# Two linear-attention and two feed-forward layers: keys of two tiles from centred rows, and weight loads on other queues

## The chip, the cores and the metric

The kernel runs on one core of a Trainium2 chip. A core has five engines with instruction queues of their own: TensorE (PE in the profile) multiplies matrices, VectorE (DVE) and ScalarE (ACT) work on tiles element by element, GpSimd (POOL) does small element-wise work and issues DMAs, and SyncE (SP) here only issues DMAs. Each engine works through its queue in order and waits on semaphores. The metric is the device time of one execution in microseconds (us); lower is better.

## The reference

The input `x` is 2048 rows of 512 values in bfloat16. Four layers follow one another: attention (A), feed-forward (B), and the same two again with the same weights.

```python
def _A_ref(x, wqkv, wo):              # D = 512, H = 32 heads of 16
    q, k, v = split_heads(x @ wqkv)
    phi = lambda t: jnp.where(t > 0, t + 1, jnp.exp(t)) + 1e-6
    pq, pk = phi(q), phi(k)
    kv  = jnp.einsum("bhsd,bhse->bhde", pk, v)
    z   = jnp.einsum("bhsd->bhd", pk)
    num = jnp.einsum("bhqd,bhde->bhqe", pq, kv)
    den = jnp.einsum("bhqd,bhd->bhq", pq, z)[..., None] + 1e-6
    return merge_heads(num / den) @ wo

def _B_ref(x, w_gate, w_up, w_down):  # inner width 1792
    return (silu(x @ w_gate) * (x @ w_up)) @ w_down

x = x + _A_ref(_layernorm(x), A_wqkv, A_wo)
x = x + _B_ref(_layernorm(x), B_w_gate, B_w_up, B_w_down)
# and both lines once more
```

The layer norm takes the mean off each row and divides by the root of variance plus 1e-5; it has no weights. The attention has no mask over positions: every query sees the sums over all keys.

## The kernel before, in words

The rows are held on the chip as sixteen tiles of 128 rows (`X`), in four groups of four tiles. Layers are numbered 0 to 3; 0 and 2 are attention, 1 and 3 feed-forward. All weights are loaded once.

*How work is named and ordered.* The kernel first records operations with what they read and write, and each engine then gets its operations in an order written out by hand: `PROGRAM` is the order of TensorE in tokens, `ORDER` has one list for each other engine. Semaphore waits follow from the recorded reads and writes. A token has the layer, a letter and the tile or group. `0t0` transposes normalised tile 0 on TensorE, `0k0` makes its keys, `0g0` adds its outer product to the accumulators, `0z0` its keys' sum. `0q03` makes queries of group 0, columns 3, and `0d03` the part of the denominators that they give. `0v` turns the outer products into per-head key-value matrices and `0m0` multiplies them by Wo. `0r0` spreads 1/denominator of group 0 over the heads' columns by matmuls, and `0w3` is the output projection of tile 3. `1u011` is gate and up of group 0, column 11, and `1n3` the down-projection of tile 3. `S` is one filler matmul of 128 columns on zeros. In `ORDER` a name has the token, a dot and the step: `0x4.apply` is the normalisation of tile 4, `0k0.exp` a step of `phi` of its keys.

*Layer norm* (`ln`): statistics on VectorE (`stats`, `aggr`) or ScalarE (`stats`, `sq`, then `negm` on GpSimd), `vpe` (variance plus epsilon), `pow` (1/std, on GpSimd) and `apply` into `xnA` (layers 0 and 2) or `xnB`. `apply` is on VectorE, or on ScalarE with one more small step, `nmr`. The normalised tile is transposed into `xnT`: by DMA, issued by SP (`xT` in SP's list), or, for tiles named in `PE_T` with a `t` (in layer 0: tiles 0, 1, 2, 3 and 14), by four TensorE transposes (`xt_pe`, line 544) and a copy out of the accumulator (`xT` on VectorE, line 552).

*Keys and queries* (`k_proj`, `q_proj`, `phi`): four matmuls of 512 columns into one accumulator bank. `phi` then takes `exp` on ScalarE (line 563), `ts` (minimum with 1, plus 1e-6, line 568) on VectorE, and the maximum with the value plus 1. That is one VectorE pass from the accumulator (`phi`, line 575), or, for names in `ON_ACT`, `id1` on ScalarE (line 566) and a shorter VectorE pass (line 572).

*Sums and denominators*: the keys' sums are masked per head into `Zm` (line 615), with `mask`, whose three building steps stand on GpSimd (`i.c5`, `i.c6`, `i.c7`; the last is line 429). In layer 0 tile 12's keys go into the sum on VectorE (`0s`: a copy and two conversions), the others by matmuls (`z`). Every `d` token needs `Zm`. Its result is inverted on VectorE (`den`). It is then spread by TensorE (`rep_pe`, with four VectorE products of line 750), for groups with a `d` in `PE_T` (0d0, 0d2, 2d1), or by four ScalarE passes (`rep`), four DMA transposes on SP (`rT`) and four VectorE products (`pqn`, line 732).

*Weight loads.* Keys' weights come on ScalarE's queue, X and the queries' weights Wq on SP's. The rest are issued by GpSimd in this order: Wv, Wo, four pairs of Wg and Wu, and four parts of Wd. The first of them waits for all transposes by DMA of layer 0. GpSimd has four DMA semaphores in turn, so each load is issued only when the one four places earlier has landed. The last step of `mask`, `i.c7`, stands behind the fourteenth load in GpSimd's list.

Of the kernel before, what the change touches and what calls it, by code (L numbers as in the profile page):

```python
# [4 lines left out]
ACT = mybir.ActivationFunctionType  # L5
# [160 lines left out]
S S S S S S S S S S S S S S S S S S S S S S S S S S S S S S S S S S S S S S S S S 0t0 0k0 S S S S S S S S S 0t1 S S  # L166
S 0t2 S S S 0k1 0g0 S 0k2 0t3 0g1 S S S 0k3 0k4 0g2 0k5 0g3 0k10 S 0g4 0k9 0g5 0k6 0k7 0q03 0g10 0z0 0k8 0k15 0z4
0g7 0k13 0k12 0k11 0g9 0z2 0z10 0z9 0q11 0z3 0z5 0z8 0t14 0z15 0g6 0z13 0k14 0q02 0z7 0q10 0q01 0q00 0z1 0g11 0q12
0q21 0z14 0z6 0z11 0q13 0s 0d02 0d03 0d01 0d00 0g8 0q20 0d11 0q22 0g13 0d12 0d13 0d10 0q23 0d20 0g15 0g12 0g14 0d23
0d22 0d21 0q30 0v 0q31 0m0 0r0 0m1 0m2 0r2 0m3 0w3 0w2 0q33 0w1 0w0 0w5 0w11 0q32 0w7 0w6 0w9 0d33 0w8 0w4 0w10  # L170
1u011 1u007 1u005 1u008 1u002 1u006 0d31 0d32 1u012 1u003 1u013 0d30 1u010 1u004 1u000 1u110 1u001 1u009 1n3 0w14
1n0 0w12 1u106 1n1 1u102 1n2 1u107 1u204 0w13 1u101 0w15 1u111 2k2 1u109 1u105 1u103 1u104 1u108 2k0 1u100 2k1 2q00
1u112 1u113 2k3 1n7 1u209 1n6 1u211 1u205 1n4 1n5 1u213 1u200 1u303 1u202 1u203 2q10 1u301 1u208 1u309 1u304 1u206
1u212 2g0 1u201 1u311 1u302 2q11 1u305 1u207 1u310 2q01 1u308 2q03 1u312 2q02 1u210 1n11 1u313 2k4 1u300 1n8 1n10
1u306 1n9 1u307 2k8 1n14 2k7 2k10 2k5 2q21 1n15 2k6 2k9 2k11 1n13 1n12 2q12 2k15 2k14 2g3 2g5 2q20 2q22 2k13 2q23
2g2 2k12 2g7 2g6 2g14 2q13 2s 2d01 2g12 2d02 2g1 2d00 2d03 2d20 2d13 2d21 2q30 2d22 2d10 2d12 2d11 2g13 2q31 2g10
2d23 2g15 2g4 2g9 2g11 2g8 2r1 2q32 2v 2q33 2m0 2m1 2m2 2m3 2d31 2d30 2w0 2w1 2w2 2d32 2w3 2w6 2w5 2w11 2d33 2w4 2w8
2w7 2w9 2w10 3u008 3u000 3u009 3u013 3u010 3u004 3u003 3u005 3u007 3u103 3u110 3u108 3u012 3u002 3u001 3u006 3u104
2w13 3u011 3n3 3u100 2w12 3n2 3n0 3u106 3u105 2w14 3u107 3u111 3n1 3u102 3u109 3u112 3u101 3u113 3n6 3n4 3n5 3n7
3u200 3u201 3u202 3u203 3u204 2w15 3u205 3u206 3u207 3u208 3u209 3u210 3u211 3u212 3u213 3n8 3n9 3n10 3n11 3u300  # L180
3u301 3u302 3u303 3u304 3u305 3u306 3u308 3u307 3u309 3u310 3u311 3u312 3u313 3n12 3n13 3n14 3n15
# [4 lines left out]
i.ld i.ld1 0x2.stats 0x2.sq 0x5.stats 0x7.stats 0k0.exp 0x5.sq 0x10.stats 0x10.sq 0k1.exp 0x7.sq 0x12.stats 0k2.exp  # L186
0k2.id1 0x15.stats 0x9.apply 0k3.exp 0x11.stats 0k4.exp 0x12.sq 0k5.exp 0x11.sq 0x15.sq 0k10.exp 0k9.exp i.c 0k6.exp
0k7.exp 0k6.id1 0q03.id1 0q03.exp 0k8.exp i.c1 i.c2 0k15.id1 0k15.exp 0k13.exp 0k12.exp 0k11.exp 0k11.id1 0q11.exp
i.c3 0k14.exp 0k14.id1 0q02.exp 0q02.id1 0q10.exp 0q01.exp 0q10.id1 0q00.exp 0q00.id1 0q12.id1 0q21.id1 0q12.exp
0q21.exp 0q13.id1 0q13.exp 0q20.exp 0q22.exp 0q23.exp 0d1.rep 0d1.rep1 0G0.evac 0G2.evac 0G3.evac 0q30.exp 0q30.id1  # L190
0q31.exp 0d1.rep2 0q31.id1 0M2.evac 0M0.evac 0M1.evac 0M3.evac 0d1.rep3 1x3.sq 0q33.exp 1x2.sq 1x3.apply 0q33.id1
1x1.sq 1x0.sq 0q32.exp 1x5.sq 0q32.id1 1x11.sq 1x7.sq 1u011.tanh 1u007.tanh 1u005.tanh 1x6.sq 1x11.apply 1u008.tanh
1x6.apply 1u006.tanh 1u002.tanh 1x7.apply 1x9.sq 1u012.tanh 1x9.apply 1u003.tanh 1u013.tanh 1x4.sq 1u010.tanh
0d3.rep 0d3.rep1 1u004.tanh 1x8.sq 1u000.tanh 0d3.rep2 1u001.tanh 1u110.tanh 1u009.tanh 1x10.sq 1x8.apply 1u102.tanh
1u106.tanh 0d3.rep3 2x0.sq 1x14.sq 2x1.sq 1u107.tanh 2x2.sq 1u204.tanh 2x3.sq 1u101.tanh 1u109.tanh 2x1.apply
1u111.tanh 1x14.apply 2k2.exp 1u105.tanh 1u103.tanh 2k2.id1 1u104.tanh 2k0.exp 1u108.tanh 2k0.id1 2k1.exp 2k1.id1
1x15.sq 2q00.id1 1u100.tanh 2q00.exp 1u113.tanh 1u112.tanh 1u209.tanh 1x12.sq 2k3.exp 2x7.sq 2k3.id1 1u211.tanh
1x13.sq 1u205.tanh 2x6.sq 2x4.sq 1u213.tanh 1u200.tanh 2x5.sq 1u303.tanh 1u202.tanh 1u203.tanh 1u301.tanh 2q10.exp
1u208.tanh 2q10.id1 1u309.tanh 1u304.tanh 1u206.tanh 1u212.tanh 1u201.tanh 1u311.tanh 1u302.tanh 2q11.id1 1u305.tanh
2q11.exp 1u207.tanh 1u310.tanh 2q01.id1 2q01.exp 1u308.tanh 2q03.id1 2q03.exp 1u312.tanh 2q02.exp 1u210.tanh  # L200
2q02.id1 1u313.tanh 2x11.sq 2k4.id1 2k4.exp 2x8.sq 1u300.tanh 2x10.sq 1u306.tanh 2x9.sq 1u307.tanh 2x10.apply
2k8.exp 2k8.id1 2x14.sq 2k7.exp 2q21.id1 2k10.exp 2q21.exp 2k5.exp 2k10.id1 2k5.id1 2k11.exp 2k6.exp 2x15.sq 2k9.exp
2x14.apply 2x13.sq 2x12.sq 2k15.exp 2q12.exp 2k14.exp 2q12.id1 2k15.id1 2q20.id1 2q20.exp 2q22.id1 2k13.exp 2k13.id1
2q23.exp 2k12.exp 2q23.id1 2q22.exp 2q13.exp 2d0.rep 2d0.rep1 2q31.exp 2d0.rep2 2q30.exp 2d0.rep3 2d2.rep 2G0.evac
2G1.evac 2G3.evac 2q32.exp 2d2.rep1 2q32.id1 2d2.rep2 2M0.evac 2M1.evac 2M3.evac 2q33.exp 2q33.id1 2d2.rep3 3x0.sq
3x1.sq 3x2.sq 3x3.sq 3x6.sq 3x5.sq 3x11.sq 3u008.tanh 3x11.apply 3x4.sq 3u009.tanh 3u000.tanh 3x7.sq 3u013.tanh
3u010.tanh 2d3.rep1 3u004.tanh 3x7.apply 3u003.tanh 3x9.sq 3u007.tanh 2d3.rep 3u005.tanh 3u103.tanh 2d3.rep2
3u108.tanh 2d3.rep3 3u110.tanh 3u012.tanh 3x8.sq 3u002.tanh 3u006.tanh 3u104.tanh 3u001.tanh 3u011.tanh 3x13.sq
3u100.tanh 3u106.tanh 3u105.tanh 3u107.tanh 3u111.tanh 3u102.tanh 3x10.sq 3u109.tanh 3x12.sq 3u112.tanh 3u101.tanh
3u113.tanh 3u200.tanh 3u202.tanh 3u201.tanh 3u203.tanh 3x14.sq 3u204.tanh 3x15.sq 3u205.tanh 3u206.tanh 3u207.tanh  # L210
3u208.tanh 3x14.apply 3u209.tanh 3u210.tanh 3u211.tanh 3x12.apply 3u212.tanh 3u213.tanh 3u300.tanh 3u301.tanh
3u303.tanh 3u302.tanh 3u304.tanh 3u306.tanh 3u305.tanh 3u308.tanh 3u307.tanh 3u310.tanh 3u309.tanh 3u311.tanh
3u312.tanh 3u313.tanh
""",
    "dve": """
i.c 0x0.stats 0x0.aggr 0x0.vpe 0x1.stats 0x0.apply 0x1.aggr 0x3.stats 0t0.xT 0x4.stats 0x1.apply 0x4.aggr 0x3.aggr
0x9.stats 0x2.apply 0t1.xT 0k0.ts 0x9.aggr 0k0.phi 0t2.xT 0x3.apply 0x4.apply 0k1.ts 0k1.phi 0x6.stats 0x5.apply
0t3.xT 0x6.aggr 0k2.ts 0x7.vpe 0x10.apply 0x14.stats 0k2.phi 0x13.stats 0k3.ts 0x14.aggr 0k3.phi 0x6.apply 0x7.apply
0k4.ts 0x8.stats 0k4.phi 0k5.ts 0x8.aggr 0x14.vpe 0x8.vpe 0x12.apply 0k5.phi 0x13.aggr 0k10.ts 0x8.apply 0x15.vpe
0k10.phi 0x15.apply 0k9.ts 0k9.phi 0k6.ts 0x13.apply 0k7.ts 0k6.phi 0k7.phi 0x11.apply 0q03.ts 0k8.ts 0k8.phi  # L220
0q03.phi 0x14.apply 0k15.ts 0k13.ts 0k15.phi 0k13.phi 0k12.ts 0k12.phi 0k12.zs 0t14.xT 0q11.ts 0k11.ts 0q11.phi
0k14.ts 0s.zh 0k11.phi 0q01.ts 0k14.phi 0q01.phi 0q00.ts 0q02.ts 0q02.phi 0q10.ts 0s.zl 0q10.phi 0z.zm 0q00.phi
0q12.ts 0q12.phi 0q13.ts 0d0.den 0q13.phi 0d0.den1 0q20.ts 0q21.ts 0q20.phi 0q21.phi 0d1.den 0q22.ts 0d1.den1
0q22.phi 0d0.den2 0q23.ts 0q23.phi 0G1.evac 0d2.den 0d2.den1 0v.mask 0d1.pqn 0d2.den2 0r0.pqn 0r0.pqn1 0r0.pqn2
0r0.pqn3 0d1.pqn1 0q31.ts 0r2.pqn 0w3.res 0r2.pqn1 0w2.res 0r2.pqn2 0r2.pqn3 0w1.res 0w0.res 1x2.apply 0d1.pqn2
1x1.vpe 0d1.pqn3 1x1.apply 0q33.ts 0w5.res 0q30.ts 0q33.phi 1x0.apply 0w11.res 0w6.res 0w8.res 0w7.res 1x5.vpe
0w10.res 0w4.res 0w9.res 1x11.vpe 1x5.apply 1x7.vpe 1u011.gst 1u011.h 1u005.gst 1u007.gst 0q32.ts 0q31.phi 1x6.vpe
0q32.phi 1u007.h 1u008.gst 1u005.h 1u008.h 1u006.gst 1u002.gst 0q30.phi 1u002.h 1u012.gst 1u006.h 1u003.gst 1u012.h
0d3.den 0d3.den1 1x4.apply 1u003.h 1u013.gst 1u010.gst 1u013.h 1u004.gst 1u010.h 1u004.h 0d3.pqn 1u000.gst 1u001.gst
1u000.h 1u001.h 1u009.gst 1u009.h 0d3.pqn2 1u110.gst 1u110.h 1n0.res 0w12.res 1n3.res 0w14.res 1x8.vpe 1x10.apply  # L230
1u106.gst 1n1.res 0d3.pqn1 1n2.res 0d3.pqn3 1u106.h 1u102.gst 2x2.vpe 1u204.gst 1u102.h 2x2.apply 1u107.gst 1u107.h
# [58 lines left out]
}  # L290

PE_T = set("""
0t0 0t1 0t2 0t3 2d1 0d0 0t14 0d2
""".split())


# [11 lines left out]
def bass_interleave_layers__linear_attn_block__swiglu_ffn__prompt_kernel(  # L308
# [20 lines left out]
    with stack:  # L329
# [65 lines left out]
        r_pq = Ring(NPQ)  # L395
        r_xb = Ring(NXB)
        r_xt = Ring(NXT)
        r_den = Ring(3)
        r_rrep = Ring(2)
        r_RT = Ring(2)  # L400
        r_th = Ring(NTH)
# [519 lines left out]
```

## Time and profile before

| What | Before |
|---|---|
| Median of three runs | 441.09 us (440.77 to 442.0) |
| The profiled execution's own time | 440.77 us |
| Its span in the profile | 439.0 us |
| TensorE busy | 420.1 us, 96% of the span |
| VectorE busy | 294.5 us, 67% |
| ScalarE busy | 199.6 us, 45% |
| GpSimd busy | 79.5 us, 18% |
| Granted TensorE clock, mean | 0.992 |
| Moved by DMA | 22.57 MB, mean 51 GB/s |

The profile is of one execution. Times within it count from the start of its span; the execution's own time is 1.77 us longer than the span. The chain that ended last is followed back from the last instruction, at each step to what released it. "Granted clock" is the share of full speed that TensorE had. A DMA has an issue, on the queue of the engine that starts it, and a landing, when its semaphore says that the data is there.

### The profile page before, as it was taken

The page shows a single profiled execution, that of the slowest core. Times are in us where ns is not written, and L with a number is a line of the kernel's source. Part 1 is how long each engine was busy: PE and PEld are TensorE (multiplying, and loading weights), DVE is VectorE, ACT ScalarE, POOL GpSimd, SP SyncE. Part 2 cuts the span into 40 slices and gives each one's busy share as a digit, 9 for nine tenths or more (in the row PEclk, how much of TensorE's full clock was granted, in tenths as well). Part 3 has the DMA queues.
Part 4 walks back from the last instruction along what each step waited for, and adds up shares of the span by engine and source line. Part 5 has one row for each costly group of instructions (what it writes and reads, how often), then busy time and mean ns, then how long its engine had stood idle before and what let it go on. Part 6 is the DMA issues. An engine that isn't in the chain of part 4 may idle for free.

```text
span 439.0 us, 6322 instructions
## 1 busy us (share of the span) xinstructions
PE 420.1 (96%) x2201; PEld 196.7 (45%) x2243; DVE 294.5 (67%) x636; ACT 199.6 (45%) x392; POOL 79.5 (18%) x205
## 2 busy tenths in 40 slices
PE   7899589999999999999999989999999999999997
PEld 6445244444444444444444444444444444444444
DVE  6976388887386756677374888887764727654762
ACT  5877276573245454445335636665412303411320
POOL 4633303410140122101023520331100100100000
PEclk9999699999999999999999999999999999999999
DMA  8439712131112003000020103313011020021001
GB/s 275 79 67 347 254 36 49 30 54 37 24 26 49 2 7 76 1 0 1 1 39 11 36 13 61 73 36 61 13 25 30 6 62 12 1 72 37 0 0 49
DMA packets 50175, 22.57 MB, mean 51 GB/s; under 512 B 43808, under 2 KB 48928, under 8 KB 50144
## 3 DMA queue, kind: packets, MB, share of 16 engines
q1 hardware_dynamic: 48160, 15.09, 15.8%
q0 software_dynamic: 1440, 6.55, 4.3%
q10 hardware_dynamic: 544, 0.52, 0.4%
q8 instruction: 18, 0.29, 0.3%
q14 instruction: 13, 0.11, 0.1%
HBM read 9.70 MB, written 2.10 MB: 27 GB/s over the span
## 4 chain that ended last, share of the span: by engine, by line
PE 79%; DMA 7%; DVE 7%; ACT 2%; issue 2%; POOL 1%; SPq 1%; DVEq 0%; POOLq 0%; ACTq 0%
PE pb L408 79%; DMA Wu<-in_B_w_up_dram 2%; DMA xnT<-xnA 2%; DMA Wo<-in_A_wo_dram 1%; DMA X<-in_A_x_dram 1%; DVE pk L575 1%; ACT etmp L563 1%; DVE pq L750 1%; DVE etmp L568 1%; DMA xnT<-xnB 1%; DVE X L762 1%; SPq L439 1%; ACT xnB L497 1%; DVE xnA L521 1%; DVE GT L627 0%
## 5 line engine op out<-in xcount | busy, mean ns | idle before, releaser
L782 ACT ACTIVATE tht<-pb 128x512 f32<-128x512 f32 x112 | 65.5, 594 | 126.9 <-PE pb L408 111.6
L408 PE MATMUL pb<-xnT,Wg 128*128 128x512 bf16 x439 | 113.3, 379 | 1.5 <-DVE vpe L506 0.9
L408 PE MATMUL pb<-xnT,Wu 128*128 128x512 bf16 x439 | 114.2, 379 | 0.5
L784 DVE SCALAR_TENSOR_TENSOR tht<-tht,pb 128x512 f32<-128x512 f32 x112 | 75.1, 684 | 49.5 <-ACT tht L782 47.2
L408 PE MATMUL pb<-Wd,hT 128*128 128x512 bf16 (+2 forms) x452 | 99.3, 372 | 0.5
L787 DVE TENSOR_TENSOR hT<-tht,pb 128x512 bf16<-128x512 f32 x112 | 74.5, 683 | 2.8
L408 PEld LDWEIGHTS pb<-Wd,hT 128*128 128x128 bf16 x462 | 44.6, 98 | 52.6 <-DVE hT L787 0.6
L408 PEld LDWEIGHTS pb<-xnT,Wg 128*128 128x128 bf16 x448 | 43.5, 98 | 53.8 <-issue 2.1
L408 PEld LDWEIGHTS pb<-xnT,Wu 128*128 128x128 bf16 x448 | 43.8, 98 | 53.1 <-DVE X L762 0.4
L563 ACT ACTIVATE etmp<-pb 128x512 bf16<-128x512 f32 x64 | 37.1, 594 | 30.0 <-PE pb L408 23.6
L510 POOL TENSOR_TENSOR rstd<-vpe,negh 128x1 f32<-128x1 f32 x64 | 36.6, 575 | 77.9 <-DVE vpe L506 75.8
L408 PE MATMUL pb<-Wqkv,xnT 128*128 128x512 bf16 x126 | 31.0, 379 | 3.1 <-DMA xnT<-xnA 1.5
L408 PE MATMUL pb<-xnT,Wqkv 128*128 128x512 bf16 x120 | 31.8, 388 | 0.5
L568 DVE TENSOR_SCALAR etmp<-etmp 128x512 bf16<-128x512 bf16 x64 | 19.3, 312 | 19.3 <-ACT etmp L563 19.2
L408 PE MATMUL pb<-pk,xnA 128*128 128x512 bf16 x125 | 31.8, 386 | 0.2
L408 PE MATMUL pb<-GT,pq 128*128 128x512 bf16 x127 | 29.9, 379 | 1.1 <-DVE pq L732 0.7
L497 ACT ACTIVATE xnB<-X,sums 128x512 bf16<-128x512 bf16 x32 | 22.9, 717 | 17.4 <-DMA xnT<-xnB 10.2
L500 POOL TENSOR_SCALAR mv<-sums 128x1 f32<-128x1 f32 x55 | 12.3, 232 | 94.6 <-DVE X L762 60.6
L810 DVE SCALAR_TENSOR_TENSOR pq<-pb,X 128x512 bf16<-128x512 f32 (+2 forms) x17 | 10.9, 657 | 24.3 <-PE pb L408 24.3
L497 ACT ACTIVATE xnA<-X,sums 128x512 bf16<-128x512 bf16 x23 | 16.5, 717 | 19.0 <-DVE X L810 19.0
L810 DVE SCALAR_TENSOR_TENSOR X<-pb,X 128x512 bf16<-128x512 f32 x16 | 11.0, 689 | 16.7 <-PE pb L408 16.7
L762 DVE SCALAR_TENSOR_TENSOR X<-pb,X 128x512 bf16<-128x512 f32 x32 | 21.2, 686 | 0.3 <-PE pb L408 0.3
(78 smaller groups left out, 312.6 us busy)
## 6 DMA issues: line engine op xcount, KB each, us to landing
out_dram<-pq SPq DMA_DIRECT2D x15, 128.0 KB, 1.8
Wg<-in_B_w_gate_dram POOLq DMA_DIRECT2D x4, 448.0 KB, 5.6
Wu<-in_B_w_up_dram POOLq DMA_DIRECT2D x4, 448.0 KB, 4.9
X<-in_A_x_dram SPq DMA_DIRECT2D x6, 256.0 KB, 5.2
Wd<-in_B_w_down_dram POOLq DMA_DIRECT2D x3, 512.0 KB, 5.6
Wqkv<-in_A_wqkv_dram ACTq DMA_DIRECT2D x2, 256.0 KB, 3.4
X<-in_A_x_dram SPq DMA_DIRECT2D x4, 128.0 KB, 3.3
Wqkv<-in_A_wqkv_dram SPq DMA_DIRECT2D x1, 512.0 KB, 6.4
```

The lines of the kernel that those rows point to most:

```text
L408: return op("pe", lambda e: e.matmul(o_ap, lhsT=lhsT, rhs=rhs, start=start, stop=stop, skip_group_check=skip), r=r, w=w, n=n)
L439: return op(q, lambda e: e.dma_start(o_ap, i_ap), r=r, w=w, after=after, dma=True, kind=kind)
L497: op("act", lambda a: a.activation(out=b_ap, in_=X[:, t, :], func=ACT.Square, scale=-float(D), bias=sums[:, t:t + 1], accum_out=mv[:, t, 1 ...
L500: op("pool", lambda p: p.tensor_scalar(out=mv[:, t, 0:1], in0=sums[:, t:t + 1], scalar1=-1.0 / D, scalar2=None, op0=ALU.mult), r=[f"sm{t}" ...
L510: op("pool", lambda p: p.tensor_tensor(out=rstd[:, t:t + 1], in0=vpe[:, t:t + 1], in1=negh[:], op=ALU.pow), r=[f"vp{t}", "negh"], w=[f"rs{ ...
L563: op("act", lambda a: a.activation(out=etmp[e][:], in_=PB[pb][:], func=ACT.Exp), r=[f"pb{pb}"], w=[f"e{e}"], kind="exp")
L568: op("dve", lambda v: v.tensor_scalar(out=etmp[e][:], in0=etmp[e][:], scalar1=1.0, scalar2=1e-6, op0=ALU.min, op1=ALU.add), r=[f"e{e}"], w ...
L762: op("dve", lambda v: v.scalar_tensor_tensor(out=X[:, t, :], in0=PB[pb][:], scalar=1.0, in1=X[:, t, :], op0=ALU.mult, op1=ALU.add, accum_o ...
L782: op("act", lambda e: e.activation(out=tht[a][:], in_=PB[pg][:], func=ACT.Tanh, scale=0.5), r=[f"pb{pg}"], w=[f"th{a}"], kind="tanh")
L784: op("dve", lambda v: v.scalar_tensor_tensor(out=tht[a][:], in0=tht[a][:], scalar=1.0, in1=PB[pg][:], op0=ALU.add, op1=ALU.mult), r=[f"pb{ ...
L787: op("dve", lambda v: v.tensor_tensor(out=hT[h][:, j, :], in0=tht[a][:], in1=PB[pu][:], op=ALU.mult), r=[f"pb{pu}", f"th{a}"], w=[f"h{h}_{ ...
L810: op("dve", lambda v, pb=pb, lo=lo, hi=hi: v.scalar_tensor_tensor(out=o_ap[:, lo:hi], in0=PB[pb][:, 0:hi - lo], scalar=0.5, in1=X[:, t, lo ...
```

## The change

- The keys of tiles 0 and 1 of layer 0 are made from rows that have only their mean taken off (`ctr`, a new VectorE step into the free buffer `pq[3]`). These are transposed by TensorE (`xt_c`, tokens `0c0` and `0c1`) and copied out by ScalarE into `pq[2]`. `phi` of these keys multiplies by 1/std in `exp` and in `id1`, both on ScalarE.
- The normalised rows of tiles 0 and 1, and of tile 14, are transposed by DMA on SP; tiles 2 and 3 still by TensorE. SP has fourteen transposes in layer 0 in place of eleven.
- Wv is loaded on SP's queue, behind Wq and ahead of the transposes, with no wait for them. GpSimd has nine loads (Wo, Wg, Wu) and then `i.c7`. The four Wd loads wait for the transposes of layer 1's first group, and stand later in GpSimd's list, among the steps of layer 1's norm.
- In layer 0, group 0's 1/denominator is spread by ScalarE and DMA in place of TensorE, and tile 12's keys' sum is made by matmuls (no `0s`). There are two buffers in place of three for denominators, and three in place of two for the spread rows.
- `PROGRAM` and all lists of `ORDER` are written anew, for all layers; other names in `ON_ACT` decide which passes ScalarE has. There are 45 filler matmuls in place of 61, of which 27 in place of 41 stand ahead of the first transpose.

```diff
-PE_T: 0t0 0t1 0t2 0t3 2d1 0d0 0t14 0d2
+PE_T: 0d2 0t2 0t3 2d1 0c0 0c1
...
-        weights.append(lambda a: dma("pool", Wqkv[:, :, 2 * D:], wq3[:, :, 2 * D:], w=["Wv"], after=a))
+        dma("sp", Wqkv[:, :, 2 * D:], wq3[:, :, 2 * D:], w=["Wv"])
...
+            if f"{L}c{t}" in PE_T:
+                op("dve", lambda v: v.tensor_scalar(out=pq[3][:, t, :], in0=X[:, t, :], scalar1=mean, scalar2=None,
+                                                    op0=sub),
+                   r=[xk, f"mv{t}"], w=[f"pq3_{t}_{i}" for i in range(TG)], kind="ctr")
...
+        def xt_c(L, t):
+            pb = bank()
+            tp = PB[pb][:].bitcast(BF16)
+            for c in range(NC):
+                op("pe", lambda e, c=c: e.transpose(out=tp[:, c * P:(c + 1) * P],
+                                                    in_=pq[3][:, t, c * P:(c + 1) * P], identity=ident[:]),
...
-        def phi(pb, dst, dk, name):
+        def phi(pb, dst, dk, name, by=1.0, rk=()):
             e = r_e.take()
-            on_act = name in ON_ACT
-            op("act", lambda a: a.activation(out=etmp[e][:], in_=PB[pb][:], func=ACT.Exp),
-               r=[f"pb{pb}"], w=[f"e{e}"], kind="exp")
+            on_act = name in ON_ACT or bool(rk)
+            op("act", lambda a: a.activation(out=etmp[e][:], in_=PB[pb][:], func=ACT.Exp, scale=by),
+               r=[f"pb{pb}", *rk], w=[f"e{e}"], kind="exp")
...
-        load_down(last)
...
+                if tok in head:
+                    head.discard(tok)
+                    if not head:
+                        load_down([xT_of[1, t] for t in range(TG) if (1, t) in xT_of])
```

GpSimd's list from the ninth load on, after the change:

```
i.ld7 i.ld8 i.c7 1x3.negm 1x3.vpe 1x3.pow ... 1x7.negm Wd.ld3 1x9.negm 1x7.vpe 1x6.negm 1x7.pow 1x11.pow Wd.ld1 Wd.ld2
```

## The prediction

> **What bounds the kernel now.** I read the slices of the span first, the chain that ended last second, then the waits, and last the stretches round the one place where these three agree.
>
> ```profile
> span 439.0 us, 6322 instructions
> PE   7899589999999999999999989999999999999997
> PEclk9999699999999999999999999999999999999999
> ```
>
> TensorE (PE) is busy in nearly every slice. It drops at the start, while tiles are normalised, and in the fifth slice (43.9 to 54.9 us), where the granted clock drops too. So the question is what the change does to the first 80 us; behind them lie 360 us of nearly gapless matmuls.
>
> The chain in order of time, for 26 to 80 us (start, length, piece):
>
> ```profile
> 30.67 0.59 issue
> 31.26 0.98 POOL Wqkv L439
> ...
> 43.57 4.26 DMA Wu<-in_B_w_up_dram
> 47.83 0.28 issue
> 48.11 0.71 POOL Wd L439
> 48.82 0.01 issue
> 48.83 0.38 POOL mask L429
> 49.20 0.02 issue
> 49.23 0.22 DVE Zm L615
> ```
>
> GpSimd (POOL) issues fourteen weight loads in a row. Each may only be issued when the load four places earlier has landed, and `mask`'s last pass stands behind them all. `Zm`, hence every denominator, needs `mask`. The waits (times, longest) say who paid:
>
> ```profile
> DVE Zm L615 <- POOL mask L429: 5.2, 1, 5.2
> ```
>
> PE ends its work at 44.65 and takes up the denominators at 49.58: 4.93 us idle. Stretches of 2 us over that place (last columns: granted clock, DMA share, GB/s):
>
> ```profile
> 44.00:46.00 2.00, 0.65 (x11) 0.35 (x8) 0.01 (x1) 2.00 (x5) 1.03 (x3) 1.00 0.88 254
> 46.00:48.00 2.00, 0.00 (x0) 0.00 (x0) 0.00 (x0) 0.07 (x1) 1.33 (x2) 0.74 0.98 358
> 48.00:50.00 2.00, 0.42 (x16) 0.45 (x17) 0.75 (x3) 0.00 (x0) 1.07 (x2) 0.50 0.98 340
> 50.00:52.00 2.00, 2.00 (x11) 0.71 (x9) 1.99 (x5) 0.00 (x0) 0.00 (x0) 0.50 0.97 344
> 52.00:54.00 2.00, 2.00 (x10) 0.81 (x9) 0.03 (x1) 0.33 (x1) 0.00 (x0) 0.55 0.24 80
> ```
>
> PE does nothing for two rows; then it is fully busy at a granted 0.50 until about 53.3. From 49.58 to 53.3 are 3.7 us at half speed, so 1.9 us are lost. The stall costs 4.9 + 1.9 = 6.8 us.
>
> **1. The loads (Wv to SP, Wd to later).** In the new order POOL issues nine loads (Wo, four Wg, four Wu) and then `mask`. Sizes and the wait for four places earlier are as they were, with Wo in Wv's place, so I read the distance off the old rows: the first load starts at 31.26, the ninth at 42.45 and takes 0.54, so `mask` starts 11.7 us after the first load and takes 0.37.
>
> When does the first load start? It waits for all transposes by DMA of layer 0, now fourteen in place of eleven, the last of tile 14. On VectorE (DVE) tile 14's `apply` stands behind the same `0q03.phi` as before, where it ran 30.16 to 30.57. Landing takes 2.43 (the last transpose, 28.09 to 30.52), waking POOL 0.74 (30.52 to 31.26): 33.75. DVE has 1.4 us less queued ahead (part 2), half of which I credit: 33.4 taken, 33.0 to 33.8. A second limit is the queue. X and Wq landed by 12.41; Wv takes as long behind them as Wq behind X, 1.44 (10.97 to 12.41), so transposes can land after 13.85. Queued ones were issued 1.31 us apart (19.08, 20.40, 21.71, 23.02): 13.85 + 14 x 1.31 + 0.74 = 32.9. By the mean spacing of all eleven landings, 1.59 (14.64 to 30.52), it is 36.8. That is the far end; I stay near 1.31, since the last ones before waited for `apply`, not for the queue.
>
> So `mask` ends at 33.4 + 11.7 + 0.4 = 45.5, and PE starts 0.38 later (49.20 to 49.58 before) at 45.9 in place of 49.58: **-3.7** (far ends -4.9, when nothing is left to wait for, and -0.3). What is left is a stall of 1.2 us. The clock fell only at 46.98, 2.3 us into the old stall, and the other idle time of 1.22 (17.12 to 18.33) left it at 1.00. I take the half-clock stretch as gone: **-1.9** (or 0).
>
> The Trainium skill, "TensorE: Matmul & The Clock Gate", Part 1, says that the gate judges activity in free-running windows of about 3.4 us and opens after such a window of work. By that rule a 1.2 us hole is safe, but the opening is less so: the first run of filler matmuls is cut from 41 to 27, estimated at 2.8 us, under one window.
>
> Wd is now issued behind the transposes of layer 1's first group; before, the last of them landed at 79.07, now some 7 us earlier. Four Wd loads took 8.9 us from first issue to last landing (44.70 to 53.64). The first down-projection comes fifteen gate/up columns of 1.73 us (two times 0.86) after that group's start, 26 us: covered by 17 us, worth nothing. Without the cover it would cost up to 8.9. POOL waits in front of the first Wd load; queued behind are means and 1/std of tiles 6, 7, 9 and later, first used twelve columns (21 us) on. Their transposes on SP wait with them, under the same cover.
>
> The Trainium skill, "SBUF — State Buffer", the section "SBUF: two separate sides", says that loads issued by GpSimd can starve while VectorE runs certain copy modes, which speaks against moving Wd into a busy VectorE. The nearest rows show no sign: with VectorE busy 1.97 of 2.00 (42 to 44), load issues took 0.54 each. By the rule Wd would land later by an unknown time, inside the same 17 us.
>
> **2. The head.** Tile 0's path to its keys was stats 0.69, aggregate 0.18, `vpe` 0.15, `pow` 0.57, `apply` 0.41, transpose, copy; now `ctr` (priced as `apply`, 0.41) follows the aggregate, and keys 0 come about 2 us sooner than 7.61. DVE ahead of tile 14 loses three copies (0.41 each), an `apply` (0.41) and two of 0.69 that become 0.41, and gains two `ctr`: -1.4. ScalarE gains three copies (0.6), an `apply` (0.81) and two `id1` (0.69). But none of this sets the end: PE idled 1.22 us up to 18.33 for tile 5's transpose, and from there to 44.65 it is full. Tile 5 is fourth in line behind Wv now: at spacings of 1.0 to 1.31 it lands at 17.9 to 19.1, against 18.29. I take **0** (-0.4 to +0.8).
>
> **3. Group 0's 1/den by DMA.** `0r0` leaves the path. Before, DVE multiplied 62.97 to 66.05 in four passes of 0.70, and PE idled 0.69, 0.67 and 0.32. In those 3.1 us PE still had 1.3 us that stay (four `m` of 0.22, `r2` 0.40). So up to -1.8; I take **-1.7**, zero if the evacuations of GT (0.60 each) take the place. The replacement, four spreads on ScalarE, four transposes (2.4 us to landing, 1.3 apart) and four `pqn` of 0.42, has 10 us between `den` (50.55) and the output projection; hidden. Without that cover it costs 5.
>
> **4. The rest.** New order in all layers, same matmuls. PE idle there was 0.92 at 79.38 and about 2.0 in five holes between 254 and 282: **0**, give or take 1.5.
>
> **Sum.** 439.0 - 3.7 - 1.9 - 1.7 = 431.7 span. That execution took 440.77, 1.77 more than its span; 433.5. The median of the runs is 441.09, 0.3 above that execution.
>
> **Rivals.** *All of the stall goes and the head gains:* transposes come at 0.95 us spacing (tiles 5 and 10 landed 0.51 apart, so it can be), PE never waits: -4.9 - 1.9 - 1.8 and -0.5 in the head; span 429.9, time 431.7. Against it: tile 14's `apply` stays late on DVE.
>
> *The first 14 us run at half clock:* the opening filler is shorter, and matmuls from 6 to 18 us, about 32 of 512 columns, take 0.43 in place of 0.22. 6.9 us more work against some 4 of idle time and filler: +3, 436.5. For: filler matmuls before 6 us ran at 0.107 spacing, later ones at 0.055. Against: filler stands between the keys.
>
> *Slower:* the transposes, not the loads, hold everything. Wv sits ahead of them in SP's queue and three more are in it. One of the eleven issues took 2.40 and tile 5 took 4.3 to land. At a mean spacing of 2.0 the first load starts at 13.85 + 28 + 0.74 = 42.6, `mask` ends at 54.7, PE goes on at 55.1: +5.5, half clock kept, -1.7 from part 3: 444.6. It decides above 1.73, where the first load comes at 38.8 (7.5 later than before: 5.8 back from five fewer loads, 1.7 from part 3). Against: six of the ten steps between issues were 1.28 to 1.32.
>
> **Numbers.** Forecast 0.63; full gain 0.13; half-clock head 0.10; slow transposes 0.07; the other layers' new order eats most of it (437 to 441) 0.07. The range 430 to 439 takes in the first three, with part 1's far end. A difference of 0.3% (1.3 us) is about what a measurement of this kernel can tell from none: faster 0.90, same 0.03, slower 0.07.
>
> **What would show it.** Right: `mask` directly behind the ninth load near 45 us; PE's hole before `Zm` about 1 us; clock 1.00 from 44 to 56; no 0.70 passes between the `KVT` mask and the first output projection; gate/up columns starting 7 us sooner, near 72; first POOL load near 33.4. Wrong: that load beyond 36, 0.50 before 18 us, or a later start of layer 2 relative to layer 1.

## The result, and the profile after

| | Before | After |
|---|---|---|
| Median | 440.93 us (439.87 to 442.0, 4 runs) | 430.5 us (430.26 to 431.57, 4 runs) |
| Ratio | | 0.9768 [0.9739, 0.9797] |
| Profiled execution, its span | 440.77, 439.0 us | 430.26, 428.5 us |

The changed kernel is 10.4 us faster; 433.5 (430 to 439) was predicted. The span fell by 10.5 us where the sum had 7.3. The result lies at the lower end of the range. Where sum and span differ can be read off the starts of the same work in both traces (us):

| From, to | Before | After | Change | Predicted |
|---|---|---|---|---|
| start to PE's last work ahead of `Zm` | 44.65 | 42.82 | -1.83 | 0 |
| PE's hole ahead of the denominators | 4.93 | 0.89 | -4.04 | -3.7 |
| denominators to `KVT` matmuls (half clock) | 10.80 | 9.02 | -1.78 | -1.9 |
| `KVT` matmuls to first output projection | 5.71 | 3.80 | -1.91 | -1.7 |
| to first gate/up | 13.29 | 12.20 | -1.09 | 0 |
| all behind it | 359.7 | 359.8 | +0.1 | 0 |

The page of the profile after (span; busy tenths of PE; granted clock):

```profile
span 428.5 us, 6269 instructions
PE   7999999999999999999999999899999999999997
PEclk9999999999999999999999999999999999999999
```

The fifth slice is full and its clock no longer falls. The chain that ended last, from GpSimd's first load to the denominators (start, length, piece):

```profile
30.99 0.60 issue
31.59 4.69 DMA Wo<-in_A_wo_dram
36.28 0.28 issue
36.56 5.66 DMA Wu<-in_B_w_up_dram
42.23 0.28 issue
42.51 0.54 POOL Wu L439
43.05 0.01 issue
43.05 0.37 POOL mask L429
43.42 0.02 issue
43.45 0.22 DVE Zm L641
```

The mechanism stands as before, only shorter: nine issues, then `mask`. It still ends the wait, though little is left of that (line of the waits: us, times, longest):

```profile
DVE Zm L641 <- POOL mask L429: 1.3, 1, 1.3
```

Stretches of 2 us over the place (PE, PEld, DVE, ACT and POOL busy; granted clock; DMA share; GB/s):

```profile
42.00:44.00 2.00, 1.10 (x15) 0.49 (x14) 0.72 (x3) 2.00 (x4) 0.90 (x2) 1.00 0.90 262
44.00:46.00 2.00, 2.00 (x24) 1.05 (x21) 1.59 (x4) 0.38 (x2) 0.00 (x0) 1.00 0.93 366
46.00:48.00 2.00, 2.00 (x25) 1.05 (x23) 1.91 (x6) 2.00 (x5) 0.00 (x0) 1.00 0.06 25
```

PE loses 0.9 us in the first row and nothing in the next two, at full clock. In the last row the DMA queues are almost empty, since no Wd load follows; this turned out to matter more than anything in the forecast (below).

PE's own line of time (start, us; in brackets the idle time before it and what ended it):

```profile
16.01 1.89 PE L408 MATMUL pb<-Wqkv,xnT 128*128 128x512 bf16 x8
...
43.71 0.59 PE L408 MATMUL pb<-Zm,pq 128*128 128x8 bf16 x16 [0.89 <-DVE Zm L641]
...
54.85 1.02 PE L408 MATMUL pb<-Wo,KVT 128*128 128x512 bf16 x4 [0.20 <-DVE KVT L695]
...
56.53 1.90 PE L408 MATMUL pb<-GT,pq 128*128 128x512 bf16 x8
...
68.73 1.03 PE L408 MATMUL pb<-xnT,Wg 128*128 128x512 bf16 x4
```

The eight matmuls at 16.01 make the keys of tiles 4 and 5, with no wait; before, those of tile 5 waited 1.22 us for its transpose. The output projection starts straight behind `KVT`, with no 0.70-us products between. Gate/up starts at 68.73, just after tile 0's transpose landed (68.25). The last two starts before, with PE's idle time ahead of them:

```profile
66.09 1.90 PE L408 MATMUL pb<-GT,pq 128*128 128x512 bf16 x8 [0.32 <-DVE pq L750]
...
79.38 0.81 PE L408 MATMUL pb<-xnT,Wg 128*128 128x512 bf16 x3 [0.92 <-DVE vpe L506]
```

### The profile page after: what moved, and what is told of

It is laid out like the page before. It is cut to its first block, busy times and chain, and to the rows that moved or that the text cites. A ratio compares the mean times of both kernels' runs of the same rounds, so it can differ in the third digit from the quotient of the medians.

```text
span 428.5 us, 6269 instructions
## 1 busy us (share of the span) xinstructions
PE 416.2 (97%) x2161; PEld 194.5 (45%) x2203; DVE 288.0 (67%) x626; ACT 204.5 (48%) x397; POOL 84.7 (20%) x212
## 4 chain that ended last, share of the span: by engine, by line
PE 81%; DMA 7%; ACT 5%; DVE 4%; issue 2%; SPq 0%; POOL 0%; POOLq 0%; DVEq 0%; ACTq 0%
PE pb L408 81%; DMA RT<-rrep 3%; DMA Wu<-in_B_w_up_dram 1%; ACT etmp L583 1%; DMA Wo<-in_A_wo_dram 1%; DMA X<-in_A_x_dram 1%; ACT rrep L745 1%; ACT pq L586 1%; DMA xnT<-xnA 1%; DVE tht L810 1%; DMA xnT<-xnB 1%; DVE pk L595 0%; DVE X L788 0%; SPq L439 0%; ACT xnA L497 0%
## 5 line engine op out<-in xcount | busy, mean ns | idle before, releaser
L408 PEld LDWEIGHTS pb<-xnT,Wg 128*128 128x128 bf16 x448 | 43.6, 98 | 53.3 <-DMA xnT<-xnB 1.1
L583 ACT ACTIVATE etmp<-pb 128x512 bf16<-128x512 f32 x62 | 36.0, 597 | 25.9 <-PE pb L408 17.5
L500 POOL TENSOR_SCALAR mv<-sums 128x1 f32<-128x1 f32 x53 | 12.4, 242 | 104.4 <-DVE X L788 56.4
L408 PE MATMUL pb<-pk,xnA 128*128 128x512 bf16 x125 | 30.8, 379 | 0.2
L408 PE MATMUL pb<-Wqkv,xnT 128*128 128x512 bf16 x117 | 29.2, 379 | 0.3 <-ACT xnT L553 0.2
L497 ACT ACTIVATE xnA<-X,sums 128x512 bf16<-128x512 bf16 x21 | 15.1, 717 | 14.1 <-DVE X L836 14.0
```

The source lines that it names most:

```text
L408: return op("pe", lambda e: e.matmul(o_ap, lhsT=lhsT, rhs=rhs, start=start, stop=stop, skip_group_check=skip), r=r, w=w, n=n)
L497: op("act", lambda a: a.activation(out=b_ap, in_=X[:, t, :], func=ACT.Square, scale=-float(D), bias=sums[:, t:t + 1], accum_out=mv[:, t, 1 ...
L500: op("pool", lambda p: p.tensor_scalar(out=mv[:, t, 0:1], in0=sums[:, t:t + 1], scalar1=-1.0 / D, scalar2=None, op0=ALU.mult), r=[f"sm{t}" ...
L583: op("act", lambda a: a.activation(out=etmp[e][:], in_=PB[pb][:], func=ACT.Exp, scale=by), r=[f"pb{pb}", *rk], w=[f"e{e}"], kind="exp")
```

## The experiments

The theory after this reading: (1) most of the gain is `mask`'s place behind fewer loads, with the half-clock stretch; (2) group 0's spread by DMA is worth 1.9 us; (3) centred keys are worth almost nothing; (4) Wd's later place counts only through `mask`. The rivals were a gain of the later loads as such, of Wv's queue, of the centred keys, or of the new order. Ratios are to the kernel before on the same chip (442.21, 441.89 and 442.0 us in the three sets).

| Kernel | us | Ratio [95%] |
|---|---|---|
| before, mask first | 435.77 | 0.9857 [0.9825, 0.9888] |
| after, Wd ahead of mask | 438.6 | 0.992 [0.9893, 0.9948] |
| before, Wv on SP | 440.65 | 0.996 [0.9941, 0.998] |
| before, filler in the hole | 442.28 | 1.0015 [0.999, 1.004] |
| after, mask first | 428.87 | 0.9703 [0.9677, 0.9728] |
| after, no centred keys | 431.33 | 0.9759 [0.9734, 0.9784] |
| after, group 0's spread by TensorE | 435.95 | 0.987 [0.9842, 0.9898] |
| after, Wv on GpSimd | 433.87 | 0.9817 [0.9787, 0.9846] |
| after, again | 429.57 | 0.9723 [0.9699, 0.9748] |
| after, mask first, Wd behind Wu | 438.32 | 0.9911 [0.9881, 0.994] |
| after, mask first, Wv on GpSimd | 431.06 | 0.9752 [0.9726, 0.9778] |
| before, mask first, group 0's spread by DMA | 441.21 | 0.9996 [0.9968, 1.0025] |

**Before, with `mask` ahead of the loads.**

```diff
-0x13.pow i.ld i.ld1 ... Wd.ld3 i.c7 1x3.negm
+0x13.pow i.c7 i.ld i.ld1 ... Wd.ld3 1x3.negm
```

> The kernel before with one thing moved: the last step of mask stands ahead of the fourteen loads in GpSimd's list, all else as it was. Theory (the stall is the mask's place behind the loads, and the half clock is its consequence): Zm follows the sums' matmuls at once, TensorE's hole at 44.65 shrinks from 4.93 to under 0.4 us, the granted clock stays at 1.00 from 44 to 56, and the span falls by 4.6 + 1.9 = 6.5 us, to 432.5 (time about 434.3, ratio 0.985). Rival (something else is nearly as late behind the mask, such as queries' phi or the loads): the hole goes, but under 3 us are gained. The first output projection should still have the four 0.70 passes of group 0 ahead of it.

One name moved in one list won 6.3 us of the 10.4 (442.21 x 0.0143; 5.0 to 7.7 by the interval). In its profile the hole is 0.46 us and the stretches that ran at half clock are full:

```profile
44.00:46.00 2.00, 1.78 (x26) 1.06 (x25) 1.25 (x4) 1.82 (x4) 0.83 (x3) 1.00 0.79 258
46.00:48.00 2.00, 1.68 (x22) 1.01 (x23) 1.86 (x6) 1.28 (x3) 1.42 (x2) 1.00 0.88 355
```

From denominators to `KVT` it took 8.97 us, as after (9.02). So part 1 of the prediction is shown, and for this gain no load had to move. This execution (437.54, the slowest of four) had the clock at 0.50 for 3.4 us from 61.76 instead, where TensorE waits for the 0.70-us products.

**After, with the Wd loads back ahead of `mask`.** Nine loads become thirteen.

```diff
-i.ld8 i.c7 1x3.negm ... 1x7.negm Wd.ld3 1x9.negm
+i.ld8 Wd.ld Wd.ld1 Wd.ld2 Wd.ld3 i.c7 1x3.negm ... 1x7.negm 1x9.negm
```

> The changed kernel with the four Wd loads back in front of mask and gated as before; Wv stays on SP. Theory: thirteen loads, mask starts about 16.4 us after the first load (17.6 with fourteen before), so near 48.0, TensorE goes on at 48.8 in place of 43.71, the hole is 5.9 us, the clock falls to 0.50 again for two windows of 3.4 us; together +5.1 and +1.9, time about 437.5. Rival (the new order of the head and of layers 1 to 3 carries the gain): at most +2, time under 432.5.

By ratio it took 6.7 us more than the changed kernel (0.992 against 0.9768; 8.7 against its second set, 0.9723). `mask` ends at 48.64, PE idles 6.2 us up to 49.01, and the clock is at 0.50 from 44.94 to 55.18, three windows of 3.41 us in place of the two expected. The waits and the clock:

```profile
DVE Zm L641 <- POOL mask L429: 6.5, 1, 6.5
```

```profile
PEclk9999599999999999999999999999999999999999
```

`KVT` to output projection stayed at 3.51 us.

**Before, with Wv on SP's queue.** One load fewer ahead of `mask`.

```diff
-weights.append(lambda a: dma("pool", Wqkv[:, :, 2 * D:], wq3[:, :, 2 * D:], w=["Wv"], after=a))
+dma("sp", Wqkv[:, :, 2 * D:], wq3[:, :, 2 * D:], w=["Wv"])
```

> The kernel before with Wv alone moved to SP's queue, behind Wq and ahead of the transposes; thirteen loads on GpSimd ahead of mask. Theory: the transposes of tiles 4 and 5 were issued at 12.10 and 13.99 and landed at 14.64 and 18.29; Wv's data is through by about 13.3, so they land as before (within 0.5), the first load on GpSimd stays near 31.3, mask comes 1.1 us sooner and TensorE's hole shrinks to 3.8; the clock still falls. Time 1.1 us less, 439.8. Rival (Wv's place delays the transposes by its 1.44 us): tile 5 lands at 19.7, the first load near 32.7, the mask as late as before; time unchanged or 0.5 more.

1.8 us were won by ratio (0.9 to 2.6 by the interval). `mask` ended 1.07 us sooner (48.12), the price of one load, and PE was ready 0.7 us sooner (43.95). Tile 4's transpose was issued at 11.52 and landed at 14.11, so Wv ahead of the transposes did not hold them: the prediction's slower rival has no ground here.

**Before, with 80 filler matmuls of 128 columns in the hole** (`F`), to keep the clock up and leave the wait.

```diff
-0q13 0s 0d02
+0q13 0s F 0d02
```

> The kernel before with 80 filler matmuls of 128 columns (about 4.5 us at full clock) in TensorE's hole, between the sums and the first denominators; the wait for mask stays. Theory: the hole costs 1.9 us beyond its own length through the half clock; with the filler the clock stays at 1.00 from 44 to 56, TensorE still goes on at about 49.6, and the span falls by 1.9 us to 437.1 (time 439.0). Rival (other engines set the pace after the hole, so that the half clock lay beside their work): clock 1.00 but under 0.5 us gained.

The clock stayed at 1.00 and denominators to `KVT` took 8.98 us in place of 10.80, so the half-clock stretch was worth 1.8 us, as priced. The stretches show the hole filled at 1.00:

```profile
46.00:48.00 2.00, 2.00 (x40) 2.00 (x37) 0.00 (x0) 0.15 (x1) 0.69 (x1) 1.00 0.90 303
48.00:50.00 2.00, 1.30 (x24) 1.12 (x21) 0.00 (x0) 0.00 (x0) 1.42 (x2) 1.00 0.98 348
```

Yet the time did not fall. In this execution `mask` ended 1.2 us later, because the loads landed later from 39 us on, and a transpose of group 1's spread took 4.15 us to land (59.12 to 63.27), so `KVT` to output projection was 7.18 us. PE stood idle there for 1.74 and 0.75 us, and a window at 0.50 followed (65.84 to 69.25). Whether the filler caused the late loads and the slow transpose is not settled.

**After, with `mask` ahead of the loads.**

```diff
-i.c6 i.ld i.ld1 ... i.ld8 i.c7 1x3.negm
+i.c6 i.c7 i.ld i.ld1 ... i.ld8 1x3.negm
```

> The changed kernel with the last step of mask ahead of the nine loads in GpSimd's list. Theory: the last 0.89 us of TensorE's hole before Zm shrinks to about 0.3 (the sums' last matmul, the Zm pass of 0.22 and the wake-ups), and 0.6 us are gained: span 427.9, time 429.9. Rival (the next late thing takes its place, group 0's spread by DMA or the queries' phi): the hole goes, the first output projection still starts at 56.5, nothing gained.

PE goes into the denominators without a wait:

```profile
41.50 1.02 PE L408 MATMUL pb<-xnT,Wqkv 128*128 128x512 bf16 x4
42.36 0.55 PE L408 MATMUL pb<-Zm,pq 128*128 128x8 bf16 x16
```

This has the lowest time of all. The changed kernel had 0.9768 and 0.9723 in its two sets, so the gain is some 1 to 3 us by ratio; against the second set the intervals overlap. The spans (426.7 against 428.5 and 427.7) say 1.0 to 1.8.

**After, with no centred keys**: tiles 0 and 1 normalised as the others and transposed by TensorE, no DMA transposes of them.

```diff
-PE_T: 0d2 0t2 0t3 2d1 0c0 0c1
+PE_T: 0d2 0t2 0t3 2d1 0t0 0t1
```

> The changed kernel without centred keys: tiles 0 and 1 are normalised, transposed by TensorE and copied by ScalarE, for keys and queries alike; no ctr, 12 transposes by DMA in place of 14, phi of keys 0 and 1 without the factor; loads, order and group 0's spread as in the changed kernel. Theory (the head's gain of 1.8 us comes from the early transposes of tiles 4 and 5, which stand 0.5 us apart behind Wv): keys 0 start near 7.4 in place of 6.1, but tile 5 still lands by 16.2 and TensorE still reaches Zm at 42.8 plus or minus 0.4; time 430.2 to 430.9. Rival (the early keys are the gain): TensorE reaches Zm 1.5 to 1.8 us later, near 44.5, time 432.2.

The ratio is that of the changed kernel. PE was ready at 43.18 against 42.82. The part of the change that is largest in the code is worth 0.4 us in the trace, and nothing that the times can tell.

**After, with group 0's 1/denominator spread by TensorE** (`0r0` back; three denominator buffers, two for spread rows).

```diff
-0m0 0m1 0m2 0m3 0r2
+0m0 0r0 0m1 0m2 0m3 0r2
```

> The changed kernel with group 0's 1/denominator spread by TensorE again (0r0 and four 0.70 passes), three denominator buffers and two spread buffers, as before; with two spread buffers the spread of group 3 is made in another order of its four tiles. Theory: the stretch from the KVT matmuls to the first output projection grows from 3.80 to 5.7 us, as it was before, and the time by 1.9 us to 432.4. Rival (ScalarE and the DMA spread had taken the place, so that undoing it frees them): under 0.7 us.

`KVT` to output projection took 5.93 us in place of 3.80: 2.1 us, as expected. The time rose by more (0.987 against 0.9768, 4.5 us). In the profile 1.1 us more lie ahead of `Zm`, with no edit there: PE waits 1.03 us at 24.03 for a DMA transpose that took 4.28 us to land, with no weight load beside it. Another 2.5 lie between the first gate/up and layer 2's `KVT`, mostly in PE's holes of 0.92 us between 115 and 119 and of 1.64 at 265.35, ended by a ScalarE spread pass. The buffers and group 3's order differed too, so what made these holes is not settled.

**After, with Wv back on GpSimd.** Ten loads ahead of `mask`.

```diff
-dma("sp", Wqkv[:, :, 2 * D:], wq3[:, :, 2 * D:], w=["Wv"])
+weights.append(lambda a: dma("pool", Wqkv[:, :, 2 * D:], wq3[:, :, 2 * D:], w=["Wv"], after=a))
```

> The changed kernel with Wv back on GpSimd as first of ten loads, nothing in front of the transposes on SP but Wq. Theory: the first transpose lands about 1.4 us sooner (near 12.9 in place of 14.30), tile 5's at 15.95 as it was, since it was issued only at 13.49; the head is unchanged; mask comes one load (1.1 us) later, TensorE's hole grows from 0.89 to 2.0 us, the clock stays at 1.00; time +1.1, 431.6. Rival (Wv in front held the head back): TensorE reaches Zm 1 us or more earlier, the first load comes 1 us sooner, and the time stays at 430.5.

It gave back 2.2 us by ratio (0.9817 against 0.9768, with intervals that overlap). `mask` ended at 44.31 (43.41), the hole was 1.6 us; the first transpose landed at 12.85 in place of 14.30, and nothing came of it: tile 5's, the fourth, was issued at 13.22 and landed at 15.64.

By then parts 1 and 3 seemed to add up. The last set was to confirm it, and did not.

**After, again**, for comparison on one chip:

> The changed kernel unedited, on the same chip as the next three, so that versions which differ by one or two us can be compared there. Expected 430.5 us (it took 430.3 to 431.6 so far), ratio 0.976 to the kernel before.

**After, `mask` first and the Wd loads straight behind Wu.** If Wd's place counts only through `mask`, this costs nothing.

```diff
-i.c6 i.ld ... i.ld8 i.c7 1x3.negm
+i.c6 i.c7 i.ld ... i.ld8 Wd.ld Wd.ld1 Wd.ld2 Wd.ld3 1x3.negm
```

> The changed kernel with the mask's last pass ahead of the loads AND the four Wd loads put back behind the Wu loads. Theory (only mask's place behind the loads cost anything; where Wd is loaded is free): same as the version with the mask first, 428.9 us, Zm straight behind PE's work near 42.4, no hole. Rival (Wd's move matters by itself): the four transposes of group 0's spread 1/den are issued from about 46 to 51 us, when the Wd loads now still move data (to about 52); a transpose among loads was seen to take 4 us in place of 2.4, so group 0's first output projection comes up to 2 us later, 430 to 431 us. KVT to first output projection 3.5 us by the theory, 4.5 to 5.5 by the rival.

The rival was right and too small: 8.75 us more than the changed kernel on the same chip. The chain:

```profile
45.64 0.53 ACT rrep L745
...
46.23 11.82 DMA RT<-rrep
58.05 0.02 issue
58.08 0.42 DVE pq L758
58.50 0.35 DVE pq L592
```

One DMA transpose, issued at 46.23 while Wd was on the way, landed after 11.82 us; most others take 2.4. Who waits for it (us, times, longest):

```profile
ACT rrep L745 <- DMA RT<-rrep: 8.9, 1, 8.9
DVE pq L758 <- DMA RT<-rrep: 8.5, 1, 8.5
PE pb L408 <- DVE pq L592: 8.3, 1, 8.3
```

There are three buffers for spread rows, so ScalarE's fourth pass waits for the first transpose to have read its buffer, and stands ahead of the later `exp`. VectorE's product (L758) waits for the same transpose and stands ahead of `phi` of the last queries (L592). PE needs those for its denominators and stands still for 8.3 us:

```profile
58.89 0.48 PE L408 MATMUL pb<-Zm,pq 128*128 128x8 bf16 x12 [8.31 <-DVE pq L592]
```

The stretches (last columns: granted clock, DMA share, GB/s) show that the loads suffer too:

```profile
46.00:48.00 2.00, 2.00 (x25) 1.10 (x24) 1.86 (x5) 1.75 (x5) 0.75 (x1) 1.00 1.06 332
48.00:50.00 2.00, 2.00 (x11) 0.89 (x10) 1.40 (x4) 1.16 (x2) 0.71 (x1) 1.00 1.11 290
50.00:52.00 2.00, 0.58 (x3) 0.09 (x1) 0.00 (x0) 0.00 (x0) 0.00 (x0) 1.00 1.22 118
52.00:54.00 2.00, 0.00 (x0) 0.00 (x0) 0.00 (x0) 0.00 (x0) 0.00 (x0) 1.00 1.08 209
54.00:56.00 2.00, 0.00 (x0) 0.00 (x0) 0.00 (x0) 0.00 (x0) 0.00 (x0) 0.90 1.26 75
```

The DMA engines are busy throughout but move 75 to 209 GB/s in place of 330. The last Wd load landed 11.1 us after its issue (48.07 to 59.18); where no transposes ran beside it, 5.7 (47.56 to 53.26, Wd ahead of `mask`).

**After, `mask` first and Wv on GpSimd.** Wv is the first of ten loads, which end one load later.

```diff
-i.c6 i.ld ... i.ld8 i.c7 1x3.negm
+i.c6 i.c7 i.ld ... i.ld9 1x3.negm
```

> The changed kernel with the mask's last pass ahead of the loads AND Wv loaded by POOL ahead of Wo, as in the kernel before. Theory (Wv's queue counted only because one load more stood ahead of the mask): same as the mask-first version, 428.9 us, within 0.7. Rival (Wv on SP has a worth or price of its own: its transfer delays the first transposes by 1 to 2 us): first transposes land near 12.9 in place of 14.3 and the time falls below 428.2, or it rises above 429.6 if the later loads are missed.

The theory missed, and the rival's second case came: 1.5 us more than the changed kernel beside it by the medians, with intervals that overlap, where 1 to 3 less had been won with `mask` first alone. The loads' end, 48.94, now lies behind the transposes' start, 46.01; the first landed after 4.78 us and PE idled 1.24 us for `phi`.

**Before, `mask` first, and group 0's spread by DMA**: parts 1 and 3 with the Wd loads where they were.

```diff
-0x13.pow i.ld ... Wd.ld3 i.c7 / PE_T: 2d1 0d0 0t14 0d2 / 0m0 0r0 0m1 / 0x11.xT 0d1.rT1
+0x13.pow i.c7 i.ld ... Wd.ld3 / PE_T: 2d1 0t14 0d2 / 0m0 0m1 / 0x11.xT 0d0.rT 0d0.rT1 0d0.rT2 0d0.rT3 0d1.rT1
```

> The kernel before with the mask's last pass ahead of the loads AND group 0's 1/den spread by ScalarE and DMA (part 3 alone, in the order of before, with the ring sizes of after). Against the kernel before with the mask first alone (435.8 us, 5.7 us from KVT to the first output projection, a half-clock window there): theory: 3.8 us there, the 0.70-us passes gone and with them the half-clock window: 1.9 us less, 433.5 to 434.0 us. Rival: the four transposes are issued from about 50 us, among the Wd loads that last till 55.5, and land late: the first output projection waits for them and nothing is won, 435.5 us or more.

The rival holds, and again by more than its number. Two edits worth -6.3 and, by the trace, about -2 gave nothing together. PE's line, and the piece of the chain that made it wait:

```profile
56.52 0.48 PE L408 MATMUL pb<-Zm,pq 128*128 128x8 bf16 x12 [4.68 <-DVE pq L575]
```

```profile
48.49 5.93 DMA RT<-rrep
```

Group 0's first transpose against the weight loads in four kernels (us):

| After, mask first, and | Issued | Last load landed | Transpose landed | It took | Output projection |
|---|---|---|---|---|---|
| nothing else | 45.94 | 46.77 | 48.34 | 2.40 | 54.84 |
| Wv on GpSimd | 46.01 | 48.94 | 50.80 | 4.78 | 56.51 |
| (before, spread by DMA) | 47.21 | 54.22 | 54.15 | 6.94 | 64.34 |
| Wd behind Wu | 46.23 | 59.18 | 58.05 | 11.82 | 65.15 |

In the two kernels with the Wd loads behind Wu, the transpose lands about when the last load does; with Wv on GpSimd it lands 1.9 us after it. A short overlap costs nothing: 0.8 us of it in the first row, and in the kernel before with `mask` first a transpose issued at 53.41 beside the last two Wd loads took 2.60 us. In the changed kernel itself the last load landed at 46.98 and the first of these transposes was issued at 47.34: the two just miss each other.

## Why the prediction was right or wrong

**Part 1** was right in its mechanism and nearly in its sum. First load to `mask` took 11.46 us (11.7), hole 0.89 (1.2). The half-clock stretch was worth 1.78 (1.9), which two kernels with the hole closed or filled confirm (8.97 and 8.98 us from denominators to `KVT`, as after). That the 1.9 came so near is partly luck: the clock's record has 0.50 from 46.95 to 53.78, not to 53.3, so 4.2 us of work lay in it and the same sum gives 2.1. The sixteen small matmuls on `Zm` lost nothing in it (0.56 us at 0.50, 0.59 at 1.00). The wrong step is the first load's start, 31.59 in place of 33.4. Tile 14's `apply` was taken to be held by its place behind `0q03.phi`, with 0.7 us of credit. But that `phi` waits for PE's queries, and both PE and VectorE came to it earlier. VectorE's line of time, before and after:

```profile
29.82 0.41 DVE L572 TENSOR_TENSOR pq<-pq,etmp 128x512 bf16<-128x512 bf16 x1
30.16 0.41 DVE L521 TENSOR_SCALAR xnA<-X,mv,rstd 128x512 bf16<-128x512 bf16 x1
```

```profile
27.14 0.68 DVE L595 SCALAR_TENSOR_TENSOR pq<-pb,etmp 128x512 bf16<-128x512 f32 x1
27.75 0.41 DVE L525 TENSOR_SCALAR xnA<-X,mv,rstd 128x512 bf16<-128x512 bf16 x1
```

`apply` is 2.4 us earlier. PE's part in this is 1.5 us (`0q03` starts at 23.79, before at 25.31), a gain in the head, which the prediction had set at 0. Also, the two steps of `0k8` (0.29 and 0.69 us) no longer stand ahead of this `phi` in VectorE's list. What each was worth was not separated.

**Part 2, the head at 0, is the step that failed**; it measured -1.83. With part 4's -1.09 this is nearly all of the 3.2 us between the sum and the span. In the head before, PE waited for tile 5's transpose:

```profile
18.34 1.04 PE L408 MATMUL pb<-Wqkv,xnT 128*128 128x512 bf16 x4 [1.22 <-DMA xnT<-xnA]
```

Tile 5, fourth in line, was priced at 17.9 to 19.1, as if the four transposes began only when Wv had landed and then followed at spacings of 1.0 to 1.31. Its transpose landed at 15.95. The first four were issued at 7.66, 9.95, 11.23 and 13.49. Three landed soon after Wv (13.83), at 14.30, 14.79 and 15.36, 0.5 to 0.6 us apart; the fourth landed 2.46 us after its own issue. 1.31 is the pace of issue on SP, and here issues ran ahead of Wv's landing. The trace of before showed two landings 0.51 apart, and the prediction put that in a rival only.

Most of the 2.3 us by which tile 5 came sooner than before has another source. Before, it was issued at 13.99, 0.5 us later, and took 4.30 us to land. The old order's traces have 4.06 to 4.35 us for this transpose in four of five, each with a PE wait of 1.0 to 1.3 us behind it. In the fifth (before, `mask` first, spread by DMA) it took 2.45, PE did not wait, and was ready at 43.32. The nine traces of the new order have 2.42 to 2.66. So the hole goes with one slow transpose; why it was slow is open, and the rest of the 1.83 was not traced.

The kernels of the experiments start from two orders, so the size can be checked: PE was ready at 43.3 to 45.9 in the four unfilled kernels with the old order and at 42.5 to 43.9 in nine with the new one; -1.5 between the means (44.45, 42.92).

**Part 3** was right for this kernel, -1.91 against -1.7, and its cover of 10 us was misjudged. The 2.4 us to landing were taken from transposes of before, which ran with hardly a weight load beside them. "Without that cover it costs 5" should have read: beside the Wd loads it costs more than 8.

**Wd at no worth** was thus the second wrong step, in its reason rather than its number. The prediction asked what Wd's later landing costs, found 17 us of cover, and that held: with issues of 0.75 to 0.83 us beside a busy VectorE, Wd was there long before the first down-projection at 94.93. It did not ask what the room left by Wd gives. With `mask` first, Wd's place decides over 9 us (428.87 against 438.32, on two chips; within one, 8.75 against the changed kernel). With Wd ahead of `mask` the time is the same, 438.6: then `mask` holds the denominators back until the loads are through, and the transposes come after.

The Trainium skill, "SBUF — State Buffer", section "SBUF: two separate sides", warns that loads issued by GpSimd can starve beside VectorE's copy modes. The changed kernel shows 0 to 0.09 us more per Wd issue than before, and no more; whether VectorE ran such a mode then is not on record.

**Part 4** at 0 is right behind 80 us, and missed -1.09 at layer 1's start. Every kernel with the new order took 12.2 to 12.4 us from output projection to gate/up, whatever else was edited, and those with the old one 12.7 to 14.3 (the longest with a half-clock window); so it belongs to the order. Which edit in it was not tried.

**The rivals.** "All of the stall goes and the head gains" came nearest (431.7): the head gained more than the 0.5 us it allowed, and only in part for its reason (landings close together), while 0.9 us of stall stayed. That it came so near is partly luck, since it had nothing for layer 1's start. "Half clock in the first 14 us" did not happen: the clock was full from 6.65 us on, with 27 filler matmuls. "Slower" did not happen at its place, 14 to 33 us; its mechanism, transposes held up behind weight loads, is the one that undoes the gain when Wd stays.

## What to carry to other kernels

Before moving a small step out from behind loads, ask what its lateness protected. Here `mask` behind the loads had kept DMA transposes and weight loads apart. Moving `mask` alone was good, and so was the spread by DMA with `mask` late (seen in the new order only); in the kernel before, the two together, with the loads in place, won nothing. Price a queued transfer by its own issue and by how close landings come, not by the pace of issues, and by rows where the same traffic runs beside it. Read a one-name move in a queue's order as carefully as the largest new function: here the one was worth 6.3 us and the other 0.4.

## What the hardware showed

*DMA transposes beside weight loads.* Three of them and the loads slowed each other until both were done: 10.0 to 11.9 us in place of 2.4, and 75 to 209 GB/s with the DMA engines fully busy. In the changed kernel two transposes of layer 1 stand beside its later Wd loads and took 3.92 and 4.71 us; PE did not wait for them. Even without loads single transposes took 4.0 to 4.5 us in many of the traces (48.58 to 52.85 after); this stayed unexplained.

*The clock gate.* The granted clock changed only on a grid of 3.41 us, and always between 1.00 and 0.50. Between 10 and 90 us of the profiled executions that have a record of the clock (all but one), each of the 12 windows in which TensorE was busy for 1.76 us or less was followed by a window at 0.50, and of those at full clock with 1.79 or more none was. At half clock, a window with 2.76 us busy was still followed by 0.50 (48.35 to 51.77 with Wd ahead of `mask`), and those with 3.07 or more by 1.00. The limit is not sharp: outside this stretch two windows with 1.62 and 1.75 us busy kept 1.00. So the hole of 4.93 us lost two windows, and holes of 0.89 and 1.24 us none. The Trainium skill, "TensorE: Matmul & The Clock Gate", Part 1, has the same free-running window, 3413 ns, but lets the clock fall after an idle one; here half a window of idleness was mostly enough.
